# Batch 0's attention written out in a fixed order, with products on zeros in each step; batch 1 takes its mask from TensorE

## The chip, the cores and the metric

The kernel runs on one core of a Trainium2 chip. The metric is the device time in microseconds (us) of one execution, the median of several. The core has five engines that the text names: TensorE (PE in the rows; PEld is its weight load), VectorE (DVE), ScalarE (ACT), GpSimd (POOL) and SyncE (SP, which here only issues transfers). Each engine runs its own instructions in order and waits on semaphores for the others. TensorE's clock has two levels, 1.2 and 2.4 GHz; the profile gives the granted clock as a share of the upper one, so 0.50 is the lower level and 1.00 the upper.

## What is computed

Four batches of 576 tokens with eight heads of 64 channels go through attention, then through a dense network with a residual, then through a routed one with eight experts.

```python
scores = scale * np.matmul(q, k.transpose(0, 1, 3, 2))
mask_local = (rel >= 0) & (rel < 32)
mask_strided = (rel >= 0) & (pos[None, :] % 32 == pos[:, None] % 32)
scores = np.where(masks[None], scores, -1000000000.0)      # heads 0-3 local, 4-7 strided
attn = np.exp(scores - np.max(scores, axis=-1, keepdims=True))
attn = attn / (np.sum(attn, axis=-1, keepdims=True) + 1e-09)
x = np.matmul(attn, v)                                     # to tokens x 512 channels
xn = (x - mu) / np.sqrt(var + 1e-06) * g_ln
x = x + np.maximum(xn @ w_ch1, 0.0) @ w_ch2                # 512 -> 2048 -> 512
...                                                        # then one of 8 experts per token
```

## The kernel before, in words

Both masks leave few keys per query, so attention is cut into blocks. A *pair* is two heads of one batch, `(b, hp)`; its queries are handled in three *units* of three or four blocks. A unit goes through five stages, each a function of its own: `st_scores` (scores into PSUM, then what DVE does to them), `st_exp` (exponentials on ACT), `st_norm` (the division by the sum), `st_trans` (transposes on TensorE and a copy back to SBUF by ACT) and `st_out` (the product with v and the copy into `xt`, the input of the dense network). Before a pair's first unit, `prep` transposes its q and k and copies them into place. All PSUM tiles of these stages share four buffers through `side`.

The dense network takes its tokens in chunks of 256. Chunk 0 is the first 256 tokens of batch 0, so its first product (`mm1`, L613) needs all four pairs of batch 0. Batch 0's attention therefore stands at the front of the program, with nothing but preparation beside it: 12 units in the order `(0, 0)`, `(0, 2)`, `(0, 3)`, `(0, 1)`. The text calls it the prologue. Batches 1 to 3 are worked into the products of the dense network by a plan of due times (`SPANS`), batch 1 beside the chunks 0 and 1. The dense weights come as 64-bit numbers and are turned into pairs of 32-bit ones in *turns* (`w_low` and `w_high` on DVE, `w_sign` on ACT, `w_split` on DVE or ACT and POOL); six turns are worked into the prologue.

Batch 0 is the only one in `FAST`. For a fast unit the mask is a product of a unit matrix with the mask on TensorE (L300), DVE takes the largest score (L316) and subtracts it (L317), and ACT does one exponential for the unit (L328). The sum of the exponentials comes from two more products with a matrix of equal numbers (L372), after which DVE adds 1e-9 (L378), takes the reciprocal of all 162 to 216 columns (L379) and multiplies while it copies into `xt` (L397). For the other batches DVE adds the mask and finds the extreme in one operation per block (L320), ACT does one exponential with a running sum per block (L331), and DVE divides on the 3 or 4 sums of a row (L340 to L342).

`keep_clock` issues products whose results nobody reads: ten at the start (`WARM0`), on a block of zeros, and two of 256 columns in each unit of batch 0 (`WARM`), on the transposed weights `pt`:

```python
if b == 0:
    keep_clock(pt...[0:n, 0:256]..., WARM)
```

The order of instructions on an engine is the scheduler's, which works from the program text and its own estimates; `keep` and `issue_after` pin single ones. SP issues the transfers of batch 0 with those of the first six weight blocks between them (`load_mixed`, `ORD`): small v transfers alternate with large weight blocks.

## Time and profile before

| | |
|---|---|
| three executions | 914.50, 916.74, 918.66 us, median 916.74 |
| the profiled execution | 914.36 us |
| its span, first to last instruction | 912.5 us |
| mean granted clock of TensorE | 0.962 |
| busy of the span: PE, PEld, DVE, ACT, POOL | 96%, 86%, 52%, 40%, 17% |
| first product of the dense network | 71.90 us |

Lengths in rows overlap where an engine starts an instruction before the one ahead of it has ended, so the distance between two starts, and not the length, is what an instruction takes of its engine. A wait is named by what ended it.

### The profile page before, as it was taken

To read this page: it belongs to the slowest core of one execution; us is meant where nothing else is said; L and a number is where in the kernel's file an instruction comes from. 1 tells how busy PE (TensorE), PEld (TensorE's weight loads), DVE (VectorE), ACT (ScalarE), POOL (GpSimd) and SP (SyncE) were. 2 spreads that over 40 slices of the span, in tenths; PEclk is the share of its full clock that TensorE was granted. 3 is DMA by queue.
4 is the path that set the end of the run, shared out by engine and by line. 5 is a ranking of instruction groups with operands and counts; after the bars stand their busy time and mean duration, and the time that the engine had idled before them with its cause. 6 is when DMAs were issued, how large, how long until landed. Compare 5 with 4: busy or idle time off the path is not lost. (4 is left out here: it accounts for less than half of the span.)

```text
span 912.5 us, 18019 instructions
## 1 busy us (share of the span) xinstructions
PE 873.2 (96%) x6644; PEld 782.2 (86%) x6644; DVE 474.3 (52%) x1560; ACT 368.9 (40%) x919; POOL 152.2 (17%) x163
## 2 busy tenths in 40 slices
PE   7888899899999999999999999999999999999994
PEld 5657888899999999899999999999877787787773
DVE  3778756537775646657555464675722134111541
ACT  2448879943354423354231212242112244222551
POOL 2013323312020020120121212020131111110100
PEclk8757989999999999999999999999999999999999
DMA  9850444310222201210000000511374364510730
GB/s 218 219 188 1 117 108 133 91 48 1 74 52 62 57 2 27 68 43 17 28 2 24 2 24 1 185 49 47 139 265 143 139 224 157 194 48 24 285 114 15
DMA packets 95024, 82.92 MB, mean 91 GB/s; under 512 B 67395, under 2 KB 75589, under 8 KB 94920
## 3 DMA queue, kind: packets, MB, share of 16 engines
q1 hardware_dynamic: 87656, 65.41, 24.2%
q0 software_dynamic: 3632, 11.11, 3.6%
q10 hardware_dynamic: 3632, 5.09, 1.6%
q8 instruction: 55, 0.90, 0.4%
q14 instruction: 49, 0.40, 0.1%
HBM read 72.08 MB, written 10.30 MB: 90 GB/s over the span
## 5 line engine op out<-in xcount | busy, mean ns | idle before, releaser
L629 PE MATMUL acc<-h,w 128*128 128x256 f32 x1728 | 246.2, 290 | 1.0 <-DVE h L616 1.0
L613 PE MATMUL ps_h<-xc,w 128*128 128x256 f32 x1728 | 242.6, 288 | 2.5 <-ACT xc L596 1.7
L613 PEld LDWEIGHTS ps_h<-xc,w 128*128 128x128 f32 x1728 | 222.7, 195 | 5.8 <-ACT xc L596 2.4
L629 PEld LDWEIGHTS acc<-h,w 128*128 128x128 f32 x1728 | 219.9, 192 | 3.6 <-DVE h L616 1.4
L615 ACT ACTIVATE h<-ps_h 128x256 fp32r<-128x256 f32 x144 | 55.6, 386 | 220.6 <-PE ps_h L613 206.1
L616 DVE SCALAR_TENSOR_TENSOR h<-ps_h,h 128x256 fp32r<-128x256 f32 x144 | 60.7, 421 | 93.7 <-ACT h L615 93.3
L1341 PE MATMUL ps_h<-wx,xs 128*128 128x512 f32 x360 | 87.6, 398 | 0.8 <-DVEq L1268 0.8
L1369 PE MATMUL ps_y<-wx,ht 128*128 128x512 f32 x360 | 85.9, 394 | 0.0
L1341 PEld LDWEIGHTS ps_h<-wx,xs 128*128 128x128 f32 x360 | 66.6, 188 | 15.8 <-DVEq L1268 1.3
L1369 PEld LDWEIGHTS ps_y<-wx,ht 128*128 128x128 f32 x360 | 66.5, 188 | 13.3
L470 POOL TENSOR_TENSOR w<-stg,w 128x512 fp32r<-128x512 f32 x32 | 45.2, 1412 | 136.1 <-ACT w L469 69.6
L1372 ACT ACTIVATE y<-ps_y,pr 128x512 f32<-128x512 f32 x19 | 13.1, 688 | 89.2 <-PE ps_y L1369 61.6
L331 ACT ACTIVATE sm<-sm,st 108x54 f32<-108x54 f32 (+1 forms) x120 | 41.4, 348 | 15.5 <-DVE st L320 15.3
L449 ACT ACTIVATE stg<-stg 128x512 f16<-128x512 f32 x32 | 43.9, 1371 | 0.7 <-DVE stg L443 0.6
L867 DVE TENSOR_TENSOR xs<-ps_tx,xs 128x512 fp32r<-128x512 f32 x15 | 10.4, 691 | 64.0 <-ACTq L1268 45.8
L1344 ACT ACTIVATE h<-ps_h 128x512 f32<-128x512 f32 x30 | 16.3, 595 | 62.0 <-PE ps_h L1341 62.0
L759 DVE TENSOR_TENSOR wx<-raw,wx 128x1024 fp32r<-128x1024 f32 x32 | 37.5, 1220 | 1.7 <-ACT wx L756 1.3
L304 PE MATMUL ps_sc<-kT,qbd 128*128 128x96 f32 (+1 forms) x280 | 34.8, 263 | 1.6 <-DVE xt L399 0.7
L304 PEld LDWEIGHTS ps_sc<-kT,qbd 128*128 128x128 f32 (+1 forms) x280 | 32.2, 182 | 2.9 <-DVE xt L399 0.9
L756 ACT CAST wx<-raw 128x1024 fp32r<-128x1024 f32 x32 | 31.8, 1061 | 5.7 <-PE acc L629 4.1
L1373 POOL DMA_INDIRECT out_dram<-y,idx x15 | 15.1, 1005 | 113.0 <-ACT y L1372 71.3
L455 DVE SCALAR_TENSOR_TENSOR stg<-stg 128x512 int32<-128x512 int32 x32 | 25.1, 785 | 15.3 <-ACT stg L450 14.9
(375 smaller groups left out, 1203.9 us busy)
## 6 DMA issues: line engine op xcount, KB each, us to landing
stg<-in_moe_w_ch_dram SPq DMA_DIRECT2D x32, 512.0 KB
raw<-in_moe_w_dram SPq DMA_DIRECT2D x16, 1024.0 KB
raws<-in_moe_w_dram SPq DMA_DIRECT2D x16, 1024.0 KB
xrows<-row ACTq DMA_DIRECT2D x9, 520.0 KB
qnat<-in_q_dram SPq DMA_DIRECT2D x48, 72.0 KB
knat<-in_k_dram SPq DMA_DIRECT2D x48, 72.0 KB
v<-in_v_dram SPq DMA_DIRECT2D x24, 72.0 KB
v<-in_v_dram SPq DMA_DIRECT2D x72, 18.0 KB
```

The source lines that it names most:

```text
L304: pe.matmul(ps[0:m, i, :], qbd[:, q0:q0 + w, :].rearrange("p s j -> p (s j)"), kT[:, k0:k0 + n], start=not fast, stop=not fast or i == ng - 1)
L331: act.activation(sm[0:m, i, :], sm[0:m, i, :], AF.Exp, bias=st[0:m, 0, i:i + 1], scale=-1.0, accum_out=st[0:m, 1, i:i + 1])
L449: keep(act.activation(t.bitcast(F16)[..., 1], f32(t[..., 1]), AF.Copy, scale=2.0 ** -112))
L470: keep(pool.tensor_tensor(w[:, 1], r, f32(w[:, 0]), op=ALU.subtract))
L613: pe.matmul(ps, w[:, a, d, o:o + 128], xcs[c][:, b_, d, :], start=(i == 0), stop=(i == 11))
L615: act.activation(h[:, 0, :], ps, AF.Relu)
L616: dve.scalar_tensor_tensor(h[:, 1, :], ps, 0.0, f32(h[:, 0, :]), op0=ALU.max, op1=ALU.subtract)
L629: pe.matmul(accs[c][d // 2][:, d % 2, :], w[:, a, f % 2, d * 128:(d + 1) * 128], h[:, b_, :], start=(f == 0 and (a, b_) == (0, 0) and d % ...
L756: act.copy(wx[i][:, 0, :], raw[i // 2][:, i % 2, :])
L759: dve.tensor_tensor(wx[i][:, 1, :], raw[i // 2][:, i % 2, :], f32(wx[i][:, 0, :]), op=ALU.subtract)
L1341: pe.matmul(hp_[fg], s_[:, a, d, :], wx[d][:, b_, 512 * fg:512 * fg + 512], start=(i == 0), stop=(i == 11))
L1369: pe.matmul(ps, s_[a][:, f, :], wx[4 + f // 2][:, b_, 512 * (f % 2):512 * (f % 2) + 512], start=(i == 0), stop=(i == 23))
```

## The change

The prologue becomes a loop that is written out: 15 steps for 12 units. Step i issues the scores of unit i, the normalisation of unit i-1, the transposes of unit i-2, the output of unit i-3 and the exponentials of unit i, and in the steps 1, 2, 4, 5, 7 and 8 the q or k of the next pair. While `pinned` is set, every instruction of TensorE, ACT and DVE is kept in this order. Each step ends with five products of 512 columns on the block of zeros, six in the steps 0 to 2; the two per unit on `pt` are gone. The weight turns stand in the steps 6 to 11.

The sums of a unit with a TensorE mask are now one DVE reduction over the exponentials (`st_norm`), followed by the same short division as in the other batches; the two products per unit with equal numbers and the wide reciprocal are gone. Units of the pairs `(0, 0)` and `(0, 2)` have mode 2: ACT reads the scores from PSUM, one exponential per block with the extreme as bias, and DVE copies the output. Mode 1, for `(0, 3)`, `(0, 1)` and all of batch 1, keeps the subtraction on DVE and one exponential; in batch 0 ACT copies its output. The factor of the scores moves into the copy of q, in all batches, with its sign turned, so that DVE looks for the least. Transposes of q and k of batch 0 take the two PSUM buffers of the dense network. Batches 2 and 3 keep mode 0.

SP issues q, k and v pair by pair, the first two weight blocks after the third and fourth pair and the other four behind.

```diff
-FAST = (0,)
+MODES = {(0, 0): 2, (0, 2): 2, (0, 3): 1, (0, 1): 1, 1: 1}
...
-NEG = -1.0e9 / SCALE
+NEG = -1.0e9
...
-SMB, SM0, PT0, TL = 2, 3, 2, 1
-WARM0, WARM, LB = 10, 2, 5
+SMB, SM0, PT0, TL = 2, 4, 2, 1
+WARM0, WARM, LB = 10, 5, 5
...
-    pe, act, dve, pool, sp = nc.tensor, nc.scalar, nc.vector, nc.gpsimd, nc.sync
...
+        def __getattr__(self, name):
+            fn = getattr(self.eng, name)
+            if not pinned[0] or name == "dma_start":
+                return fn
+            return lambda *args, **kw: tc.keep_in_program_order(fn(*args, **kw))
+
+    pe, act, dve = Pin(nc.tensor), Pin(nc.scalar), Pin(nc.vector)
+    pool, sp = nc.gpsimd, nc.sync
...
-    pool.affine_select(out=mask_loc, in_=mask_loc, pattern=[[-2, 128]], compare_op=ALU.is_ge, fill=NEG, base=2 * STR, channel_multiplier=1)
...
+    pool.affine_select(out=mask_loc, in_=mask_loc, pattern=[[-2, 128]], compare_op=ALU.is_ge, fill=-NEG, base=2 * STR, channel_multiplier=1)
...
-            ps = side_r([128, 3 * QT], "ps_tr")
+            ps = (ps_m.tile([128, 512], F32, tag="m", name="ps_tr")[:, 0:3 * QT] if b == 0 else side_r([128, 3 * QT], "ps_tr"))
...
-                act.copy(dst(qbd[0:64, 0:S, 0]), s_[0:64])
...
+                act.activation(dst(qbd[0:64, 0:S, 0]), s_[0:64], AF.Copy, scale=-SCALE)
+                if half and b:
+                    act.activation(dst(qbd[64:128, 0:S, 1]), s_[64:128], AF.Copy, scale=-SCALE)
+                else:
+                    dve.tensor_scalar(dst(qbd[64:128, 0:S, 1]), s_[64:128], -SCALE, None, op0=ALU.mult)
...
-        fast = b in FAST
+        mode = mode_of(b, hp)
...
-        if fast:
+        if mode:
...
-        if fast:
-            mx = st[0:m, 0, 0:ng]
-            return [lambda: dve.tensor_reduce(mx, ps[0:m], axis=AX.X, op=ALU.max),
-                    lambda: dve.tensor_tensor(sm[0:m], ps[0:m], mx.unsqueeze(2).to_broadcast([m, ng, n]), op=ALU.subtract)]
+        sms[b, hp, u0] = (sm, st, ps)
+        mn = st[0:m, 0, 0:ng]
+        if mode:
+            new = [lambda: dve.tensor_reduce(mn, ps[0:m], axis=AX.X, op=ALU.min)]
+            if mode == 1:
+                new.append(lambda: dve.tensor_tensor(sm[0:m], ps[0:m], mn.unsqueeze(2).to_broadcast([m, ng, n]), op=ALU.subtract))
+            return new
...
-            dve.tensor_tensor_reduce(sm[0:m, i, :], ps[0:m, i, :], mask(i), -SCALE, 3.0e38, ALU.add, ALU.min, st[0:m, 0, i:i + 1])
+            dve.tensor_tensor_reduce(sm[0:m, i, :], ps[0:m, i, :], mask(i), 1.0, 3.0e38, ALU.add, ALU.min, st[0:m, 0, i:i + 1])
...
-        if b in FAST:
-            act.activation(sm[0:m], sm[0:m], AF.Exp, scale=SCALE)
+        mode = mode_of(b, hp)
+        if mode == 1:
+            act.activation(sm[0:m], sm[0:m], AF.Exp, scale=-1.0)
             return
         for i in range(ng):
-            act.activation(sm[0:m, i, :], sm[0:m, i, :], AF.Exp, bias=st[0:m, 0, i:i + 1], scale=-1.0, accum_out=st[0:m, 1, i:i + 1])
+            act.activation(sm[0:m, i, :], (ps if mode else sm)[0:m, i, :], AF.Exp, bias=st[0:m, 0, i:i + 1], scale=-1.0, **({} if mode else dict(accum_out=st[0:m, 1, i:i + 1])))
...
-        if b in FAST:
-            return []
-        return [
+        todo = [
             lambda: dve.tensor_scalar(rs, rs, 1e-9, None, op0=ALU.add),
             lambda: dve.reciprocal(rs, rs),
             lambda: dve.tensor_tensor(sm[0:m], sm[0:m], rs.unsqueeze(2).to_broadcast([m, ng, n]), op=ALU.mult),
         ]
+        if mode_of(b, hp):
+            todo.insert(0, lambda: dve.tensor_reduce(rs, sm[0:m], axis=AX.X, op=ALU.add))
+        return todo
...
-        ps = side([128, 2, ng, w] if fast else [128, 1, ng, w], "ps_o")
+        ps = side([128, ng, w], "ps_o")
...
-        if fast:
-            for j in range(2):
-                pe.matmul(ps[64 * j:64 * j + 64, 1], mean_w[0:n, 0:64], pt[0:n, :, j::2], start=True, stop=True)
-        if b == 0:
-            keep_clock(pt.rearrange("p g m -> p (g m)")[0:n, 0:256].bitcast(BF16).rearrange("p (n w) -> p n w", w=2)[:, :, 1], WARM)
...
-        if fast:
-            rs = pt.rearrange("p g m -> p (g m)")[:, 0:ng * w]
-            dve.tensor_scalar(rs, ps[:, 1].rearrange("p g q -> p (g q)"), float(DM), 1e-9, op0=ALU.mult, op1=ALU.add)
-            dve.reciprocal(rs, rs)
...
-            if fast:
-                dve.tensor_tensor(dst, cut(o), cut(rs), op=ALU.mult)
-            else:
-                (dve.tensor_copy if i % 2 else act.copy)(dst, cut(o))
+            (dve.tensor_copy if (i % 2 if b else mode_of(b, hp) > 1) else act.copy)(dst, cut(o))
...
-    def weights_next():
-        for fn, i in turns[nw[0]] + joins[nw[0]]:
+    def weights_turn():
+        for fn, i in turns[nw[0]]:
             fn(i)
         nw[0] += 1
+
+    joined = [0]
+
+    def weights_join():
+        while joined[0] < nw[0]:
+            for fn, i in joins[joined[0]]:
+                fn(i)
+            joined[0] += 1
+
+    def weights_next():
+        weights_turn()
+        weights_join()
...
-    load_qk(*pairs[0])
-    load_v0(0)
-    load_qk(*pairs[1])
-    big = [hold(load_w, 0), hold(load_w, 1), hold(load_qk, *pairs[2]), hold(load_w, 2), hold(load_w, 3), hold(load_qk, *pairs[3]), hold(load_w, 4), hold(load_w, 5)]
-    small = [hold(load_v0, i) for i in range(1, 4)]
-    for n in ORD:
-        load_mixed(sum((big[i] for i in n[0]), []), sum((small[i] for i in n[1]), []))
+    for i in range(4):
+        load_qk(*pairs[i])
+        load_v0(i)
+        if i > 1:
+            load_w(i - 2)
+    for i in range(2, W_START):
+        load_w(i)
...
-    while pos[0] < NSTEP or any(fifo.values()):
-        i = pos[0]
...
+    pinned[0] = True
+    us = [(b, hp, u0) for b, hp in pairs[:4] for u0, _ in GROUPS[hp]]
+    for nm in "qk":
+        prep(*pairs[0], nm)
+        keep_clock(idle, 2)
+    for i in range(len(us) + 3):
+        new, old = st_scores(*us[i]) if i < len(us) else [], st_norm(*us[i - 1]) if 0 < i <= len(us) else []
+        for p in old + new:
+            p()
+        if 1 < i < len(us) + 2:
+            st_trans(*us[i - 2])
+        if i > 2:
+            st_out(*us[i - 3])
+        if i < len(us):
+            st_exp(*us[i])
+        weights_join()
+        if i < 9 and i % 3:
+            prep(*pairs[i // 3 + 1], "qk"[i % 3 - 1])
+        keep_clock(idle, WARM + (i < 3))
+        if i > 2 and us[i - 3] == (0, 1, 0):
+            ln_0()
+        if i > 2 and us[i - 3] == (0, 1, 3):
+            ln0 = [ln_2, ln_split]
+        if i > WI and nw[0] < W_START:
+            weights_turn()
         if ln0:
             ln0.pop(0)(0)
+    weights_join()
+    pinned[0] = False
     pos[0] = NSTEP
```

What this does to the order, first on TensorE in the prologue, one unit of the pair `(0, 2)` (`ps_sc` scores, `ps_pt` transposes, `ps_o` output, `idle_ps` products that nobody reads). Before:

```order
L300 LDWEIGHTS iw
L300 MATMUL ps_sc<-mask_str,iw 108x216
L304 MATMUL ps_sc<-spare 108x54 x4
L350 MATMUL ps_pt<-iw,first 96x128 x3
L369 MATMUL ps_o<-first,v_174 64x64 x6
L372 MATMUL ps_o<-first,mean_w 64x192 x2
L285 LDWEIGHTS first
L285 MATMUL idle_ps<-first 128x256
```

With the change (line 84 is the wrapper that pins):

```order
L84 LDWEIGHTS iw
L84 MATMUL ps_sc<-mask_str,iw 108x216
L84 MATMUL ps_sc<-spare 108x54 x4
L84 MATMUL ps_pt<-iw,first 96x128 x3
L84 MATMUL ps_o<-first,v_174 64x64 x6
L84 LDWEIGHTS spare
L84 MATMUL idle_ps<-spare 128x512
```

The products with `mean_w` are gone, and what follows the output reads `spare`, the block of zeros, instead of `first`, which holds `pt`; four more such pairs follow.

On DVE, in the pair `(0, 3)` and after it (`st` sums and extremes, `xt` the output). Before:

```order
L378 TENSOR_SCALAR first<-ps_o 128x216
L317 TENSOR_TENSOR first<-ps_sc,st 128x288
L379 RECIPROCAL first<-first 128x216
L316 TENSOR_REDUCE st<-ps_sc 128x3
L397 TENSOR_TENSOR xt_331<-ps_o,first 128x12x8
L397 TENSOR_TENSOR xt_362<-ps_o,first 128x12x8
L397 TENSOR_TENSOR xt_387<-ps_o,first 128x12x2
L317 TENSOR_TENSOR first<-ps_sc,st 128x288
```

With the change:

```order
L84 TENSOR_REDUCE st<-first 108x4
L84 TENSOR_SCALAR st<-st 108x4
L84 RECIPROCAL st<-st 108x4
L84 TENSOR_TENSOR first<-first,st 108x216
L84 TENSOR_REDUCE st<-ps_sc 108x4
L84 TENSOR_TENSOR first<-ps_sc,st 108x216
L84 COPY xt_361<-ps_o 128x12x8
L84 COPY xt_397<-ps_o 128x12x8
L84 COPY xt_445<-ps_o 128x12x2
```

The wide reciprocal has gone; a reduction and two operations on four columns stand ahead of a product, and all of it comes before the next unit's scores are looked at.

On SP, behind the loads of the first pair, before:

```order
L191 DMA qk<-in_q_dram 96x6x64 x2
L191 DMA qk<-in_k_dram 96x6x64 x2
L191 DMA stg<-in_moe_w_ch_dram 128x4x256
L191 DMA v_189<-in_v_dram 18x11x64
L191 DMA stg<-in_moe_w_ch_dram 128x1024
L191 DMA v_189<-in_v_dram 18x11x64
L191 DMA qk<-in_q_dram 96x6x64
```

With the change, from the third pair on:

```order
L205 DMA qk<-in_q_dram 96x6x64 x2
L205 DMA qk<-in_k_dram 96x6x64 x2
L205 DMA v_196<-in_v_dram 18x11x64 x2
L205 DMA v_196<-in_v_dram 18x10x64
L205 DMA v_196<-in_v_dram 18x11x64 x2
L205 DMA v_196<-in_v_dram 18x10x64
L205 DMA stg<-in_moe_w_ch_dram 128x4x256
```

The q and k of the third pair stood behind two weight blocks and now stand ahead of all of them.

## Rows read from the trace of the kernel before

**Rows 1.** The page, busy tenths in 40 slices of the span: TensorE
```profile
PE   7888899899999999999999999999999999999994
```

**Rows 2.** Busy us of each engine by stretch, then granted clock, DMA share, GB/s
```profile
14.00:31.00 17.00, 16.14 (x107) 12.56 (x108) 8.17 (x18) 5.03 (x14) 0.00 (x0) 0.50 1.06 237
31.00:41.30 10.30, 8.83 (x107) 6.25 (x105) 7.92 (x22) 5.16 (x12) 0.00 (x0) 1.00 0.95 251
41.30:71.90 30.60, 25.58 (x167) 16.30 (x168) 24.46 (x51) 13.23 (x22) 5.65 (x4) 0.50 0.47 153
71.90:78.60 6.70, 6.36 (x24) 5.66 (x25) 6.40 (x13) 4.96 (x9) 1.64 (x1) 0.50 0.01 2
98.00:188.00 90.00, 80.88 (x718) 76.40 (x718) 53.01 (x202) 78.22 (x192) 29.92 (x23) 0.96 0.42 114
```

**Rows 3.** Timeline of TensorE before 80 us: start, length, line, operation, count
```profile
1.22 4.45 PE L285 MATMUL idle_ps<-spare 128*128 128x512 bf16 x10 [1.22 <-DVE spare L926]
...
7.26 0.30 PE L300 MATMUL ps_sc<-mask_loc,iw 128*128 128x96 bf16 x2
...
8.44 0.29 PE L300 MATMUL ps_sc<-mask_loc,iw 128*128 128x288 bf16 x1
...
9.21 0.29 PE L300 MATMUL ps_sc<-mask_loc,iw 128*128 128x288 bf16 x1
...
9.97 0.41 PE L265 MATMUL ps_tr<-iw,qk 96*128 96x96 f32 x3
...
48.27 0.42 PE L300 MATMUL ps_sc<-mask_loc,iw 128*128 128x288 bf16 x1
...
49.72 0.75 PE L350 MATMUL ps_pt<-iw,first 108*54 108x108 f32 x3
...
71.90 1.94 PE L613 MATMUL ps_h<-xc,w 128*128 128x256 f32 x6 [1.73 <-ACT xc L596]
```

**Rows 4.** Timeline of TensorE from 137 to 159 us
```profile
137.39 0.49 PE L350 MATMUL ps_pt<-iw,sm 128*96 128x128 f32 x3
137.72 0.81 PE L304 MATMUL ps_sc<-kT,qbd 128*128 128x96 f32 x6
...
147.25 0.66 PE L265 MATMUL ps_tr<-iw,qnat 96*128 96x96 f32 x6
147.69 1.07 PE L629 MATMUL acc<-h,w 128*128 128x256 f32 x7
...
158.25 0.57 PE L369 MATMUL ps_o<-pt,v 96*64 96x64 f32 x12
158.75 0.50 PE L613 MATMUL ps_h<-xc,w 128*128 128x256 f32 x2
```

**Rows 5.** Timeline of DVE, copy into the first 256 tokens
```profile
67.90 0.42 DVE L397 TENSOR_TENSOR xt<-ps_o,first 128x64 f32<-128x64 f32 x2
```

**Rows 6.** Groups by line and shape, 0 to 78 us: busy, mean ns, idle before
```profile
L379 DVE RECIPROCAL first<-first 128x192 f32<-128x192 f32 x6 | 8.1, 1344 | 0.1
...
L449 ACT ACTIVATE stg<-stg 128x512 f16<-128x512 f32 x6 | 8.2, 1358 | 0.1
...
L450 ACT ACTIVATE stg<-stg 128x512 f32<-128x512 f32 x6 | 4.0, 668 | 0.1
...
L316 DVE TENSOR_REDUCE st<-ps_sc 128x3 f32<-128x288 f32 x6 | 2.7, 447 | 2.8 <-PE ps_sc L304 2.8
...
L328 ACT ACTIVATE first<-first 128x288 f32<-128x288 f32 x6 | 2.5, 448 | 6.4 <-DVE first L317 6.4
```

**Rows 7.** Groups by line and shape, 78 to 440 us
```profile
L331 ACT ACTIVATE sm<-sm,st 128x96 f32<-128x96 f32 x54 | 19.8, 370 | 11.4 <-DVE st L320 11.2
...
L331 ACT ACTIVATION_READ_ACCUMULATOR sm<-sm,st 128x1 f32 x54 | 10.3, 191 | 0.0
...
L342 DVE TENSOR_TENSOR sm<-sm,st 128x288 f32<-128x288 f32 x18 | 8.2, 453 | 0.2
...
L340 DVE TENSOR_SCALAR st<-st 128x3 f32<-128x3 f32 x18 | 3.9, 215 | 7.6 <-ACT sm L331 7.1
```

**Rows 8.** Waits of TensorE from 98 to 188 us, longest in total first
```profile
PE ps_tr L265 <- DVE qbd L277: 2.8, 2, 2.3
PE ps_o L369 <- ACT pt L358: 1.3, 1, 1.3
PE ps_var L549 <- ACT pt L358: 1.2, 1, 1.2
```

More of the change, by code (lines that the diff above doesn't have):

```diff
@@ L72, in attention_moe_moe, with __init__ @@
     nc = tc.nc
-    pe, act, dve, pool, sp = nc.tensor, nc.scalar, nc.vector, nc.gpsimd, nc.sync
+    pinned = [False]
+    class Pin:
+        def __init__(self, eng):
+            self.eng = eng
+        def __getattr__(self, name):
[5 more added lines that the diff above has]
+    pool, sp = nc.gpsimd, nc.sync
     def f32(ap):
@@ L275, in prep @@
             else:
-                act.copy(dst(qbd[0:64, 0:S, 0]), s_[0:64])
-                (act.copy if half and b else dve.tensor_copy)(dst(qbd[64:128, 0:S, 1]), s_[64:128])
+                act.activation(dst(qbd[0:64, 0:S, 0]), s_[0:64], AF.Copy, scale=-SCALE)
[3 more added lines that the diff above has]
+                    dve.tensor_scalar(dst(qbd[64:128, 0:S, 1]), s_[64:128], -SCALE, None, op0=ALU.mult)
     sms, pts = {}, {}
@@ L303, in st_scores @@
             k0 = max(0, q0 - STR) if hp < 2 else q0
-            pe.matmul(ps[0:m, i, :], qbd[:, q0:q0 + w, :].rearrange("p s j -> p (s j)"), kT[:, k0:k0 + n], start=not fast, stop=not fast or i == ng - 1)
+            pe.matmul(ps[0:m, i, :], qbd[:, q0:q0 + w, :].rearrange("p s j -> p (s j)"), kT[:, k0:k0 + n], start=not mode, stop=not mode or i == ng - 1)
         if b == 0:
@@ L368, in st_out @@
             for j in range(2):
[L369 to L379 removed]
+                pe.matmul(ps[64 * j:64 * j + 64, i, 0:k], vv[0:min(n, k) if hp > 1 else n, i, j, :], pt[0:min(n, k) if hp > 1 else n, i, j:2 * k:2], start=True, stop=True)
+        o = ps.rearrange("p g q -> p (g q)")
         i = 0
```

40 lines of the change are left out of this document (8 added, 32 removed).

## The prediction

> **What bounds the kernel now.** I read the page first. From the ninth of its 40 slices on, some 180 us after the start, TensorE is busy all the time, and only the earlier slices fall below that [rows 1], so whatever brings forward the dense network's first product brings forward the end by about as much. That product starts at 71.90 us [rows 3]. Next the table by stretch [rows 2], where two things stand. TensorE's clock was granted at the lower level, 1.2 GHz, from 14 to 31 us and again from 41.3 to 78.6 us, and at the upper, 2.4 GHz, only in the 10 us between; and in the low stretches it was busy 16.1 of 17 and 25.6 of 30.6 us. So the prologue is bound by TensorE at half clock for the larger part, and by DVE in the rest (24.5 of 30.6 us). The groups by line show what DVE spends itself on: the wide reciprocal takes 1.34 us of each of six units [rows 6], and the others are as wide. Last I read the stretch of batch 1, 98 to 188 us: TensorE idles there for 9.1 of 90 us while ACT is busy 78.2 [rows 2], and its longest waits are for ACT and DVE [rows 8]. After that it hardly idles.
>
> **Term 1, the prologue.** The new loop has 15 steps in a fixed order, so I work out how long a step is for each engine, with the clock at the upper level.
>
> TensorE: the mask product and the scores of a unit take 0.77 us from one mask product to the next [rows 3], the transposes 0.33, six transposes of a q or k 0.44, the output 0.50 [rows 4]. The five products on zeros have no row at the upper level. Ten of them took 4.45 us at the start [rows 3], 0.445 each, which is 512 columns at 1.2 GHz; at 2.4 GHz I take half, 0.22, so 1.1 per step. Sum 2.7, with a q or k 3.15.
>
> The loop between DVE and ACT: DVE looks for the extreme (0.447 [rows 6]), ACT takes three exponentials (at most 0.370 each, the row that also keeps a running sum [rows 7]), DVE reduces over them, then two operations on three columns and a product. The reduction over SBUF has no row; it lies between the short operation's 0.215 and the product's 0.453 [rows 7], and I take the 0.447 of the same shape in PSUM. The reciprocal on three columns I take like the other short one. That is 0.45 + 1.11 + 0.45 + 0.22 + 0.22 + 0.45 = 2.9. In mode 1 a subtraction and one exponential of 0.448 [rows 6] replace the three: 2.7.
>
> ACT in the steps 7 to 11, where a weight turn lies: sign work 1.36 + 0.67 [rows 6], the exponential 0.45, the copy of the transposes and two or three output copies, for which I take four times 0.3, bounded by 0.2 and 0.45 from the short and the long operations above: 3.7, or 3.3 with the lower bound.
>
> The three engines lie within 2.7 and 3.7 of each other, and none waits for another inside one step, since the transposes and outputs belong to older units. I take 3.3 us a step; the range is 2.8 (nothing but the loop) to 4.1 (ACT's 3.7 and a wait ahead of it).
>
> The first mask product stood at 7.26 us [rows 3]; four products on zeros are put ahead of it, 0.9, so 8.2. Twelve steps reach 47.8, step 12 reaches 51.1. In step 13 the transposes, the output and a copy (0.33 + 0.50 + 0.32) bring the last of the first 256 tokens at 52.3. From there to the first dense product I take what it takes now, from the end of the copies at 68.3 [rows 5] to 71.9, which is 3.6, and 0.4 because five products on zeros now stand ahead of the mean on TensorE: 56.3. **That is 15.6 us less**; with the bounds of a step, 13 of which lie on the path, it is between 5.2 (4.1 us each) and 22.1 (2.8 us each).
>
> What else is moved costs nothing as long as its cover holds. SP: the DMA share is full until 31 us at some 240 GB/s [rows 2]; q, k and v of batch 0, 3.5 MB, so land by about 17 us and the six weight blocks (0.52 MB each) by about 30, as today. The first weight block is wanted in step 6 (28 us) and lies behind three pairs only; the last is wanted in step 11 (44 us). The tightest are q and k of the second pair, wanted in step 1 at about 11 us; in the trace their transposes start at 9.97 without a wait for a transfer [rows 3], and the same loads stand ahead of them as before. If that cover were gone, TensorE would stand still behind them, as the order is pinned. The factor in q's copy changes no count of operations, in batches 2 and 3 it lies beside a TensorE that is never idle: nothing.
>
> **Term 2, the clock at the first dense products.** They ran at the lower level for 6.7 us [rows 2]. TensorE's 6.4 busy us could halve, 3.2 less; but DVE is busy 6.4 us of the same stretch and the first products wait for its halves of the input. Between 0 and 3.2 I take 1.0, nearer to DVE's row.
>
> **Term 3, batch 1.** ACT loses 40 exponentials with a running sum (0.370 + 0.191 each [rows 7], 22.4 us) and gets 12 of 0.448, 5.4 us: 17 less of its 78.2. DVE gets about as much as it loses. TensorE gets 14 mask products, whose price I bound by nothing (hidden in the idle time) and the 0.29 of their length [rows 3]: 1.8 us is taken. Of the 9.1 us of idle time some 2.8 hang on DVE's copy of q and the rest mostly on ACT [rows 8]; I take that 4 go. Net 2 us less, from 7 less to 4 more.
>
> **The sum.** 914.36 - 15.6 - 1.0 - 2.0 = 895.8 against the profiled execution's own time. That execution lies 2.4 us under the median of 916.74, so I forecast a median of **898 us**.
>
> **The clock as the trace shows it, and a rule.** All of term 1 stands on the upper level. In the trace the ten full products at the start were followed by the upper level (0.29 for 288 columns at 8.44, against 0.42 at 48.27 [rows 3]). It fell at 14 us after TensorE had stood waiting for copies, and then stayed low through 17 us in which TensorE was busy 95% of the time, though with products of 54 to 96 columns on parts of the array [rows 2]. The new products are as wide as those at the start and take a third of each step, which none of the low stretches has. The Trainium skill (TensorE: Matmul & The Clock Gate, Part 1) says that the throttled state is the default and that sustained activity releases it. By that rule a TensorE that is busy throughout would win the clock back soon whatever it computes, so the second rival below could not last. This trace disagrees: 14 to 31 us was busy and low.
>
> **The rivals.**
>
> *The order costs more than it hides* (0.13). With everything pinned, one late copy holds an engine that has other work ready, as the scheduler's freedom is gone. For it: the three engines lie close together, so a slip of one is a slip of all. Against it: each stage has a step of slack. Steps of 4.1 us give 8.2 + 13 x 4.1 + 5.2 = 66.7 for the first product, 5.2 less than now: about 908.5.
>
> *The clock stays low for most of the prologue, and the products on zeros become the bound* (0.06): this is the slower side. At 1.2 GHz scores with their mask take 1.45 (48.27 to 49.72 [rows 3]), the transposes up to 0.75, the output and the six transposes up to twice the above (1.0 and, in half of the steps, 0.9), the five products 2.2: 5.6 a step, 2.3 more than at the upper level. The gain of 15.6 is gone when 7 of the 15 steps run low; all 15 give 34.5 more, so 19 us slower in the prologue, less 2 for batch 1: 934. For it: the trace has two long low stretches under a busy TensorE. Against it: the width of the new products.
>
> *The clock falls once, in the weight steps* (0.08), where steps grow to ACT's 3.7 and the last units have no scores: seven low steps eat term 1, batch 1 still gives 2 or 3, so about 914: no change.
>
> *Batch 1 gives all its idle time back* (0.10): 9 less there and not 4, and 3.2 in term 2: about 891, or 888 if the steps reach 3.1.
>
> That the change does nothing is no rival: the wide reciprocal and the products for the sums do leave the order.
>
> **How the numbers follow.** The forecast has 0.63, spread over 892 to 905 by the bounds of a step; the first and last rival lie at its two ends. The range of 887 to 910 holds the forecast, most of the last rival and most of the first: 0.8 or a little more. A measurement of this kernel tells some 0.5%, 4.6 us, from no change. Faster by more than that: 0.63 + 0.13 + 0.10 = 0.86. Within it: 0.08. Slower: 0.06.
>
> **What would show it.** Right: a granted clock near 1.00 from 10 us to the first dense product, that product at 54 to 59 us, mask products of the prologue about 3.3 us apart, less idle time of TensorE in the stretch of batch 1, and the rest unchanged in length. Wrong: mask products 5 us or more apart at 0.50 (second rival), 4 us apart at 1.00 with TensorE waiting for ACT or DVE (first rival), or a first product at 56 us with its gain lost later, while weights are being turned.

## The result and the profile after

The changed kernel takes 902.17 us (median of four executions, 900.97 to 903.65) against 916.94 us before (four, 914.50 to 918.66): ratio 0.9842, 95% interval 0.9813 to 0.987. The forecast was 898 us with a range of 887 to 910: the sign and the range hold, and the gain is 14.8 us where 18.6 were summed up. In a later comparison the same kernel took 907.4 us (six executions, 903.0 to 908.86), ratio 0.9878 with interval 0.9839 to 0.9916; why it varies is one of the findings below.

The profiled execution took 902.98 us, its span is 901.2 us and the mean granted clock 0.983. On the page, the rows that answer to [rows 1], TensorE and its clock:

```profile
PE   8989888999999999999999999999999999999995
...
PEclk9999999899999999999999999999999999999997
```

The table by stretch, to be read against [rows 2]; the columns are the same. The first call:

```profile
14.00:31.00 17.00, 15.44 (x153) 10.85 (x151) 11.81 (x42) 7.67 (x26) 0.00 (x0) 1.00 1.07 266
31.00:41.00 10.00, 10.00 (x112) 7.58 (x112) 9.14 (x29) 7.72 (x17) 1.40 (x1) 1.00 0.99 260
41.00:57.00 16.00, 13.05 (x120) 8.12 (x117) 12.91 (x29) 11.24 (x27) 4.24 (x3) 1.00 0.50 159
```

In this profile the clock stays at its upper level through the whole prologue, where it stood at 0.50 for 17 and then 30.6 us before [rows 2]. TensorE's timeline shows the steps (all pinned instructions have the line of the helper, L84) and the first dense product, now L636:

```profile
8.37 0.29 PE L84 MATMUL ps_sc<-mask_loc,iw 128*128 128x96 bf16 x2
...
16.12 0.26 PE L84 MATMUL ps_sc<-mask_str,iw 108*108 108x216 bf16 x1
...
17.93 0.93 PE L84 MATMUL ps_sc<-spare 128*108 128x54 f32 x8 [1.55 <-ACT spare L84]
...
20.72 0.26 PE L84 MATMUL ps_sc<-mask_str,iw 108*108 108x216 bf16 x1
...
42.95 0.29 PE L84 MATMUL ps_sc<-mask_loc,iw 128*128 128x288 bf16 x1
...
48.28 0.53 PE L84 MATMUL ps_pt<-iw,first 128*96 128x128 f32 x3 [1.89 <-DMA stg<-in_moe_w_ch_dram]
...
56.91 3.41 PE L636 MATMUL ps_h<-xc,w 128*128 128x256 f32 x24
```

From the first mask product at 8.37 to the twelfth at 42.95 lie 11 steps, 3.14 us each. The first dense product starts at 56.91 us instead of 71.90 [rows 3]: 15.0 us earlier. The span shrank by 11.3 us only, so something is given back behind it. To find where, I counted the products into `ps_h`, the tile of that product (2152 in each trace, the first 1728 of them of L613 before and L636 now), and compared the start of the 1st, the 73rd and the 289th. The table has the experiments too; they are told below. A ratio is to runs of the kernel before in the same comparison, of which there were four (the change; e1 to e4; e5 to e8; e9 to e12).

| kernel | 1st, us | 73rd | 289th | 73rd to 289th | ratio to before, 95% interval |
|---|---|---|---|---|---|
| before | 71.90 | 97.58 | 190.29 | 92.7 | 1 |
| changed | 56.91 | 78.85 | 177.14 | 98.3 | 0.9842 [0.9813, 0.987] |
| changed, again (e11) | 59.18 | 81.12 | 179.27 | 98.2 | 0.9878 [0.9839, 0.9916] |
| e1 no products on zeros in the steps | 62.78 | 86.19 | 184.38 | 98.2 | 0.9907 [0.9884, 0.993] |
| e3 before, with products on zeros | 65.28 | 91.67 | 185.19 | 93.5 | 0.9932 [0.9908, 0.9956] |
| e5 order left to the scheduler | 62.83 | 84.78 | 182.69 | 97.9 | 0.9889 [0.9857, 0.992] |
| e6 sums of batch 0 as before | 62.79 | 86.29 | 182.58 | 96.3 | 0.9896 [0.9854, 0.9938] |
| e4 transfers in the old order | 59.18 | 81.13 | 179.27 | 98.1 | 0.9864 [0.9844, 0.9885] |
| e2 batch 1 as before | 57.26 | 79.20 | 168.95 | 89.8 | 0.9813 [0.9787, 0.9839] |
| e7 no added 1e-9 | 54.44 | 76.36 | 168.53 | 92.2 | 0.9755 [0.9724, 0.9786] |
| e9 the same, batch 0 alone | 54.10 | 76.06 | 177.63 | 101.6 | 0.9812 [0.9779, 0.9845] |
| e10 the same, batch 1 alone | 57.21 | 79.14 | 176.26 | 97.1 | 0.9816 [0.9777, 0.9854] |
| e8 e2 and e7 together | 54.46 | 76.39 | 167.07 | 90.7 | 0.9748 [0.9715, 0.9781] |
| e12 e8, k of the second pair by DVE | 53.68 | 75.59 | 167.65 | 92.1 | 0.9715 [0.9683, 0.9748] |

Against before, the lead of the changed kernel is 15.0 us at the 1st product, 18.7 at the 73rd, 13.15 at the 289th, up to 14.3 between that and the last one, and 13.19 there. So the later stages pass on about what lead there is; another 1.9 us are lost behind the last of them. There TensorE waits 2.05 us for ACT in both kernels, and the 24 products that follow take longer now, first before, then changed:

```profile
892.91 5.73 PE L1369 MATMUL ps_y<-wx,ht 128*128 128x512 f32 x24
```

```profile
879.72 7.34 PE L1395 MATMUL ps_y<-wx,ht 128*128 128x512 f32 x24
```

These 24 products take 5.7 us in eight of the fourteen profiles and 7.1 to 7.3 in six; e3, the kernel before with products on zeros, is one of the six, and e4 is not. So most of the 1.9 us is a fall of the clock that comes in some executions, and no part of the change.

One caution for what follows: the prologue of the changed kernel stands unaltered in e2, e10 and e11, with the first product at 57.26, 57.21 and 59.18 us. One prologue so varies by 2.3 us from one execution to the next.

What is won and lost lies in three places: the prologue (-15.0), the first 72 products (25.7 us before, 21.9 now: -3.7), and the stretch in which batch 1's attention and the turning of the weights lie beside the products (92.7 before, 98.3 now: +5.6).

### The profile page after: what moved, and what is told of

The parts are those of the page before. It is cut to its first block, busy times and chain, and to the rows that moved or that the text cites. A ratio compares the mean times of both kernels' runs of the same rounds, so it can differ in the third digit from the quotient of the medians.

```text
span 901.2 us, 17965 instructions
## 1 busy us (share of the span) xinstructions
PE 867.3 (96%) x6668; PEld 777.3 (86%) x6668; DVE 474.5 (53%) x1520; ACT 365.6 (41%) x879; POOL 152.2 (17%) x163
## 5 line engine op out<-in xcount | busy, mean ns | idle before, releaser
L636 PE MATMUL ps_h<-xc,w 128*128 128x256 f32 x1728 | 239.6, 287 | 0.0
L636 PEld LDWEIGHTS ps_h<-xc,w 128*128 128x128 f32 x1728 | 221.6, 194 | 1.7
L639 DVE SCALAR_TENSOR_TENSOR h<-ps_h,h 128x256 fp32r<-128x256 f32 x144 | 60.6, 421 | 94.2 <-ACT h L638 93.5
L460 ACT ACTIVATE stg<-stg 128x512 f16<-128x512 f32 x27 | 37.2, 1377 | 0.6 <-DVE stg L454 0.6
L354 ACT ACTIVATE sm<-sm,st 108x54 f32<-108x54 f32 (+1 forms) x80 | 27.6, 347 | 13.5 <-DVE st L342 13.4
L1384 DVE TENSOR_TENSOR ht<-ps_th,ht 128x512 fp32r<-128x512 f32 x30 | 19.3, 685 | 24.5 <-ACT ht L1383 24.1
L324 PE MATMUL ps_sc<-kT,qbd 128*108 128x54 f32 (+1 forms) x240 | 30.5, 267 | 0.0
L892 DVE SCALAR_TENSOR_TENSOR pr<-io_e,e_rep,xg 128x8 f32<-128x8 f32 x15 | 3.4, 226 | 51.2 <-ACT y L1398 46.0
```

The lines of the kernel that those rows point to most:

```text
L324: pe.matmul(ps[0:m, i, :], qbd[:, q0:q0 + w, :].rearrange("p s j -> p (s j)"), kT[:, k0:k0 + n], start=not mode, stop=not mode or i == ng - 1)
L354: act.activation(sm[0:m, i, :], (ps if mode else sm)[0:m, i, :], AF.Exp, bias=st[0:m, 0, i:i + 1], scale=-1.0, **({} if mode else dict(acc ...
L460: keep(act.activation(t.bitcast(F16)[..., 1], f32(t[..., 1]), AF.Copy, scale=2.0 ** -112))
L636: pe.matmul(ps, w[:, a, d, o:o + 128], xcs[c][:, b_, d, :], start=(i == 0), stop=(i == 11))
L639: dve.scalar_tensor_tensor(h[:, 1, :], ps, 0.0, f32(h[:, 0, :]), op0=ALU.max, op1=ALU.subtract)
```

## The experiments

### The prologue: clock, order and sums

**e1: no products on zeros in the steps.**

```diff
-        keep_clock(idle, WARM + (i < 3))
```

> The changed kernel without the products on zeros inside its steps (the ten at the start and the four between the first transposes stay); nothing else differs. Theory A (the clock): the steps are short because these products hold TensorE at the upper level. Without them the granted clock is 0.50 for most of 12 to 60 us; a step on TensorE is then 1.45 (scores and mask at the lower level) + 0.75 + 1.0 + half of 0.9 = 3.65 us, up to 4.1, and the first dense product comes at 62 to 68 us instead of 56.9: ratio 0.990 to 0.996. Rival B (the order): the fixed order and the shorter DVE work make the gain, and the products on zeros only take 1.1 us a step from TensorE. Then the clock stays high or a step stays at 3.3 us, the first dense product comes at 57 us or before, and the ratio is 0.984 or lower.

Measured: 908.07 us, ratio 0.9907, first dense product at 62.78. The table by stretch of this run:

```profile
14.00:31.00 17.00, 13.83 (x99) 11.80 (x97) 9.43 (x32) 6.88 (x23) 0.00 (x0) 0.52 1.04 260
31.00:41.00 10.00, 10.00 (x86) 8.69 (x84) 7.34 (x28) 5.19 (x11) 0.00 (x0) 0.50 1.06 278
41.00:57.00 16.00, 14.40 (x100) 11.61 (x99) 15.35 (x35) 12.53 (x27) 5.64 (x4) 0.50 0.32 92
```

Theory A: the clock is low from 14 us on, and stays low through 10 us in which TensorE never pauses. But only 5.9 of the 15.0 us go (3.6 if e11's 59.18 is taken for the changed kernel); 9.1 remain at the lower clock.

**e3: the kernel before, with products on zeros.**

```diff
-    def keep_clock(t, n):
+    def keep_clock(t, n, pin=lambda x: x):
...
-            pe.matmul(idle_ps[:, 0:t.shape[-1]], t[:, 0:128], t, start=True, stop=True)
+            pin(pe.matmul(idle_ps[:, 0:t.shape[-1]], t[:, 0:128], t, start=True, stop=True))
...
-            keep_clock(pt...[0:n, 0:256]..., WARM)
+            keep_clock(idle, 5, tc.keep_in_program_order)
```

> The kernel before, with one edit: behind each of batch 0's outputs five pinned products on zeros of 512 columns in the place of the two of 256 columns on the transposed weights. Theory A (the clock): the granted clock is near 1.00 from about 25 us on to the first dense product. The order and DVE's wide reciprocals stay, and DVE's 0.8 busy share in the low stretch bounds what comes of it: the first dense product at 63 to 67 us instead of 71.9, ratio 0.990 to 0.995. Rival B (the order): the clock is not what holds this prologue, and 12 times five products of 0.22 to 0.45 us, less the 24 left out, put 10 us or more on TensorE: the first product at 75 us or later, ratio 1.003 or more.

Measured: 911.83 us, ratio 0.9932, first dense product at 65.28, 6.6 us earlier than before. Two rows of its table by stretch:

```profile
31.00:41.00 10.00, 9.49 (x107) 6.49 (x107) 8.78 (x21) 4.18 (x10) 0.00 (x0) 1.00 0.80 220
41.00:57.00 16.00, 13.86 (x137) 8.76 (x134) 15.23 (x36) 8.97 (x15) 2.84 (x2) 1.00 0.82 233
```

In these two stretches the clock is as high as in the changed kernel (from 14 to 31 us it was 0.80), and DVE is busy 15.2 of the last 16 us: now the old sums bind. Rival B, that such products only cost, falls: they are worth 6.6 us in the old order (e3) and 3.6 to 5.9 in the new (e1).

**e5: only the products on zeros pinned, the rest left to the scheduler.**

```diff
-            pe.matmul(idle_ps[:, 0:t.shape[-1]], t[:, 0:128], t, start=True, stop=True)
+            tc.keep_in_program_order(pe.matmul(idle_ps[:, 0:t.shape[-1]], t[:, 0:128], t, start=True, stop=True))
...
-    pinned[0] = True
+    pinned[0] = False
```

> The changed kernel with nothing of batch 0 pinned but the products on zeros; the scheduler orders the rest on every engine. Theory of the forecast: the fixed order is what keeps a step at 3.3 us; the first rival said it costs more than it hides. So far: products on zeros alone took 6.6 us off the first dense product, order and arithmetic without them 9.1. If the fixed order is most of those 9.1, this run has its first dense product at 61 to 65 us and a ratio of 0.988 to 0.994. Rival: the shorter DVE work and not the order is what counts; then it stands at 55 to 59 us and the ratio at 0.981 to 0.987.

Measured: 906.93 us, ratio 0.9889, first dense product at 62.83: 5.9 us later than with the fixed order (3.6 against e11), as the first theory has it. The longest wait of TensorE in this prologue shows one thing that the fixed order does:

```profile
PE ps_tr L279 <- DMA qk<-in_q_dram: 4.2, 1, 4.2
```

The scheduler has put transposes of a later pair ahead of other work, and TensorE stands 4.2 us until their q has landed. The changed kernel has no such wait in its prologue. The clock falls about this wait too (0.70 on the mean from 14 to 31 us), so this run doesn't part the order from the clock: what it loses holds both.

**e6: the sums of batch 0 as before, in the new order.**

```diff
-MODES = {(0, 0): 2, (0, 2): 2, (0, 3): 1, (0, 1): 1, 1: 1}
+MODES = {0: 1, 1: 1}
...
+                pe.matmul(po[64 * j:64 * j + 64, 1], mean_w[0:n, 0:64], pt[0:n, :, j::2], start=True, stop=True)
...
+            dve.reciprocal(rs, rs)
...
+                dve.tensor_tensor(dst, cut(o), cut(rs), op=ALU.mult)
```

> The changed kernel with batch 0's softmax sums as before: TensorE's two products per unit against a constant, DVE's wide scale and reciprocal and the product with it at each output copy; order, products on zeros and loads as changed, every unit with DVE's subtraction and one exponential. DVE then has in a step 0.45 + 0.45 for extreme and subtraction, 0.3 to 0.45 for the scale, 1.34 for the reciprocal and two or three products of 0.25 to 0.45 each: 3.4 to 3.9, and beside q's copies and weights up to 4.8. If DVE's arithmetic bounds the prologue: first dense product at 61 to 66 us, ratio 0.988 to 0.995. Rival: the order alone hides DVE's longer work: first product at 56 to 59 us, ratio 0.983 to 0.987.

Measured: 907.59 us, ratio 0.9896, first dense product at 62.79. The row of its late steps:

```profile
41.00:57.00 16.00, 13.16 (x122) 7.71 (x119) 15.52 (x35) 8.82 (x13) 4.76 (x4) 1.00 0.79 241
```

The clock is up and DVE is full (15.5 of 16 us): DVE's arithmetic binds, the rival falls. The pairs `(0, 0)` and `(0, 2)` also get DVE's subtraction back, so this tries DVE's arithmetic as a whole, and not the sums alone.

So with any one of the three parts taken away, about 9 us of the prologue's gain remain. Each costs 5.9 us of 15.0 by the first profile and 3.6 of 12.7 by e11; the three sum to more than the whole by the one and to less by the other, so whether a part is worth more beside the other two is not shown.

**e4: transfers in the order of before.** The list of loads is that of the kernel before, with `load_mixed` and `ORD`.

```diff
-    for i in range(4):
-        load_qk(*pairs[i])
...
+    for n in ORD:
+        load_mixed(sum((big[i] for i in n[0]), []), sum((small[i] for i in n[1]), []))
```

> The changed kernel with the transfers issued in the order of before (weight blocks 0 to 3 ahead of and between the third and fourth pair of q and k). By the forecast the new order of loads is worth nothing: every block lands ahead of the step that wants it, so the ratio stays at 0.984 (0.981 to 0.987) and the first dense product at 57 us. Rival: in a pinned order a late transfer stops everything behind it; the third pair lands 4 us later and v of the second pair with it, TensorE waits for transfers in steps 3 to 8, the clock may fall there, and the first product comes 1 to 6 us later: 0.986 to 0.992.

Measured: 904.09 us, ratio 0.9864, first dense product at 59.18, with the clock at 0.90 from 14 to 31 us. By itself this looked like a cost of 2.3 us, though TensorE waits for no transfer in it. But e11, the changed kernel again, has its first product at the same 59.18 and the ratio 0.9878. The new order of loads is worth nothing that these runs can show.

### Batch 1, and one short operation

**e2: batch 1 as before.**

```diff
-MODES = {(0, 0): 2, (0, 2): 2, (0, 3): 1, (0, 1): 1, 1: 1}
+MODES = {(0, 0): 2, (0, 2): 2, (0, 3): 1, (0, 1): 1}
```

> The changed kernel with batch 1's mask, extreme and sums as they were before (one DVE operation adds the mask and finds the extreme, ACT's exponentials keep the sums); batch 0 is as changed. Theory of the forecast's third term: the new form of batch 1 is worth 2 us, so without it the ratio rises from 0.984 to 0.986 or 0.987, and TensorE waits more for ACT between 57 and 180 us. Rival: in the changed kernel the stretch from the first dense product to the 289th of its line took 120.2 us against 118.4 before, and its longest wait there, 2.3 us, is for the product that ends DVE's new chain of reduce, add, reciprocal and product; so the new form gives back what it saves on ACT. Then the old form of batch 1 is as fast or faster: ratio 0.979 to 0.984, and that stretch takes 116 to 119 us.

Measured: 900.26 us, ratio 0.9813 (five executions, 895.02 to 902.68; the profiled one is the fastest). The intervals of this and of the changed kernel overlap, so the times alone don't settle it; the stretch from the 73rd to the 289th product does. One row each, before, changed, and e2:

```profile
97.58:190.29 92.71, 83.59 (x749) 78.92 (x748) 54.38 (x206) 79.49 (x195) 30.47 (x23) 0.96 0.42 116
```

```profile
78.85:177.14 98.29, 88.41 (x756) 82.92 (x754) 65.26 (x162) 73.86 (x130) 32.03 (x24) 0.91 0.40 116
```

```profile
79.20:168.95 89.75, 81.74 (x742) 76.77 (x740) 57.17 (x206) 79.73 (x196) 31.66 (x24) 0.98 0.44 125
```

With the new form ACT is less busy by 5.6 us and DVE more by 10.9; TensorE idles 9.9 us instead of 9.1, and its clock is lower, so its work itself takes longer. In the table above the stretch takes 89.8 to 93.5 us in all five profiles with the old form (before, e2, e3, e8, e12) and 96.3 to 101.6 in eight of the nine with the new form; only e7, which drops a short operation, has 92.2. On the mean of these profiles that is 97.5 us with the new form and 91.7 with the old: it costs some 6 us there. Only 0.8 us of the changed kernel's loss is idle time of TensorE. An estimate from the granted clock has most of the rest: 0.91 over 98.3 us and 0.96 over 92.7 are about 18 and 7 us at the lower level, and 10 us more at half speed are 5 us. What the new form does to DVE is to be seen in its groups by line over this stretch (line, operation, count, then busy us and mean ns of one), first before, then changed:

```profile
L342 DVE TENSOR_TENSOR sm<-sm,st 128x288 f32<-128x288 f32 (+2 forms) x12 | 5.0, 416 | 0.3
```

```profile
L363 DVE TENSOR_TENSOR sm<-sm,st 128x288 f32<-128x288 f32 (+2 forms) x12 | 9.6, 804 | 0.3
...
L366 DVE TENSOR_REDUCE st<-sm 128x3 f32<-128x288 f32 (+2 forms) x12 | 4.8, 402 | 4.2 <-ACT sm L351 4.2
...
L361 DVE TENSOR_SCALAR st<-st 128x3 f32<-128x3 f32 (+2 forms) x12 | 2.6, 219 | 0.3
```

The same product takes 804 ns where it took 416: seven of the twelve now start while POOL is subtracting weights, and these take 0.62 to 1.59 us; before, none took over 0.46. And it ends TensorE's longest wait of the stretch in the changed kernel:

```profile
PE ps_pt L374 <- DVE sm L363: 2.3, 1, 2.3
PE ps_o L392 <- ACT pt L382: 1.8, 2, 1.0
```

That this product and this wait bring the clock down is not shown. e7 below keeps both, and its stretch is short and its clock up:

```profile
76.36:168.53 92.17, 83.96 (x755) 78.96 (x754) 64.29 (x150) 73.38 (x130) 31.55 (x24) 0.96 0.43 122
```

```profile
L362 DVE TENSOR_TENSOR sm<-sm,st 128x288 f32<-128x288 f32 (+2 forms) x12 | 9.9, 826 | 0.3
```

```profile
PE ps_pt L373 <- DVE sm L362: 2.2, 1, 2.2
```

**e7: without the addition of 1e-9.** A sum holds the exponential of its own extreme, which is 1, so adding 1e-9 changes no float32 value.

```diff
-            lambda: dve.tensor_scalar(rs, rs, 1e-9, None, op0=ALU.add),
```

> The changed kernel without the addition of 1e-9 to the softmax sums, in all four batches (a sum is at least 1, so that it changes no float32 value). It takes one short DVE operation per unit, 0.17 us and up to 0.9 beside POOL's weight split, out of the chain from the exponentials to the transposes. Theory: in the steps from 8 on and in batch 1 that chain is what TensorE waits for, so the first dense product comes 0.5 to 1.5 us earlier, the waits for DVE in batch 1 shrink, and the ratio goes from 0.984 to 0.979 to 0.983. Rival: the operation lies beside other waits (ACT's turns of weights): ratio 0.983 to 0.986.

Measured: 893.89 us (six executions, 893.38 to 897.0), ratio 0.9755: 8.3 us less than the changed kernel's 902.17 (13.5 less than its 907.4 in e11), more than expected. What the operation did in the prologue is to be seen in the changed kernel's timeline of DVE and POOL at the late steps:

```profile
45.92 0.42 DVE L84 TENSOR_SCALAR stg<-stg 128x512 int32<-128x512 int32 x1
46.08 1.41 POOL L481 TENSOR_TENSOR w<-stg,w 128x512 fp32r<-128x512 f32 x1 [2.73 <-DVE w L84]
46.25 0.45 DVE L84 TENSOR_REDUCE st<-first 128x3 f32<-128x288 f32 x1
46.73 0.78 DVE L84 TENSOR_SCALAR st<-st 128x3 f32<-128x3 f32 x1
...
47.55 0.18 DVE L84 RECIPROCAL st<-st 128x3 f32<-128x3 f32 x1
...
47.76 0.46 DVE L84 TENSOR_TENSOR first<-first,st 128x288 f32<-128x288 f32 x1
```

On three columns it takes 0.78 us, ending with POOL's subtraction at 47.5. The answer for the tile of the sums (least, median and greatest ns of one) has its other lengths:

```profile
L84 DVE TENSOR_SCALAR st<-st x12: 169/171/921, 11.2 to 50.9; 128x3 f32<-128x3 f32 x6, 108x4 f32<-108x4 f32 x4, 108x3 f32<-108x3 f32 x2
```

So 0.17 is the rule, and 0.78 to 0.92 what it takes in the four steps in which it starts while POOL is subtracting. In batch 1's stretch (78.85 to 177.14 us) it takes 0.16 to 0.17 us in eleven of twelve cases. DVE's whole step here, from 44.00 to 48.14, is 4.14 us. Without it (e7) the product meets POOL in its place, and the wait of TensorE at this point shrinks from 1.89 to 0.95 us. (The changed kernel's row at 48.28 names a transfer for it, but the transposes read what DVE's product finished at 48.22, and e2, e4 and e10 name DVE for the same wait.)

```profile
44.44 1.41 POOL L480 TENSOR_TENSOR w<-stg,w 128x512 fp32r<-128x512 f32 x1 [2.31 <-DVE w L84]
...
45.09 0.18 DVE L84 RECIPROCAL st<-st 128x3 f32<-128x3 f32 x1
...
45.31 0.86 DVE L84 TENSOR_TENSOR first<-first,st 128x288 f32<-128x288 f32 x1
...
46.22 0.53 PE L84 MATMUL ps_pt<-iw,first 128*96 128x128 f32 x3 [0.95 <-DVE first L84]
```

**e9 and e10: the same in batch 0 alone (below), in batch 1 alone (`b == 1`).**

```diff
+        if b == 0:
+            todo.pop(0)
```

> The changed kernel without the addition of 1e-9 in batch 0 alone. Leaving it out everywhere gave 8.3 us, of which the prologue shows 2.5 (first dense product at 54.4 instead of 56.9). Theory: the prologue's 2.5 are batch 0's and the rest batch 1's, ratio 0.980 to 0.983. Rival: the rest is not the operation's length either but where the batch 1 work falls after an earlier start: then this run has it all, 0.974 to 0.978.

> The changed kernel without the addition of 1e-9 in batch 1 alone; first dense product at 56.9 us as in the changed kernel. Theory: batch 1's shorter chain is worth the other 5 to 6 us, through fewer falls of the clock between 57 and 180 us: ratio 0.977 to 0.980. Rival: it is worth nothing there (ACT and the weights set the pace): 0.982 to 0.986.

Measured: 900.9 us for each, ratios 0.9812 and 0.9816, beside 0.9878 for the changed kernel in the same comparison (e11). So each gives about 0.006, and both together about the 0.012 that e7 (from the other comparison) has against e11; but the intervals of both overlap that of e11, so neither is clear by itself. e9's ratio is the one that its theory gave, and the prologue's 2.8 us are there (54.10). In its profile they are lost again behind the 73rd product (101.6 us), but that execution is the slowest of its six (903.83, the others 899.38 to 901.18). e10's ratio lies between its two theories.

**e8: batch 1 as before and no addition of 1e-9.**

> The changed kernel with batch 1's old form (as in the run with ratio 0.981) and without the addition of 1e-9 to the sums in all batches. If both gains are of the same kind (a shorter chain from scores to transposes keeps TensorE from waiting, and so the clock up), they add: ratio 0.975 to 0.980. If the addition costs nothing, 0.979 to 0.984.

Measured: 893.23 us, ratio 0.9748, beside e7's 0.9755 in the same comparison: not told apart. It was expected that the two gains add; e7 alone has as much as both. Once the addition is gone, these runs tell no difference between the forms of batch 1. Why, is not shown.

**e11: the changed kernel again**, without an edit.

> The changed kernel again, beside the next three. In its first profile the products 217 to 288 of the first dense line took 35.8 us, with the clock down to 0.50 there, against 30 to 32 in every other profile. If that is a fixed collision of this order, it stands here again: 35 us or more, ratio 0.981 to 0.987. If it is chance, the stretch takes 30 to 33 us, and the profiled execution comes out at 895 to 898 us.

Measured: 907.4 us, ratio 0.9878, first dense product at 59.18. The slow part that the first profile had between the 217th and the 289th product (35.8 us) is not there (32.3), so it is no fixed part of this order, though e9's profile has it again (35.9). But the execution is no faster, and the 895 to 898 us expected of it did not come: the clock fell elsewhere (0.90 from 14 to 31 us, 0.93 from the 73rd to the 289th product). TensorE's timeline at the wait that the changed kernel had at 48.28:

```profile
49.82 0.53 PE L84 MATMUL ps_pt<-iw,first 128*96 128x128 f32 x3 [1.89 <-DMA stg<-in_moe_w_ch_dram]
...
50.87 2.31 PE L84 MATMUL idle_ps<-spare 128*128 128x512 bf16 x5
```

and the same place in the first profile:

```profile
49.25 1.25 PE L84 MATMUL idle_ps<-spare 128*128 128x512 bf16 x5
```

After the same wait of 1.89 us, five products on zeros take 2.31 us here and 1.25 there: the clock fell in one execution and not in the other. In e2, e4 and e10, behind the same wait, they take 2.18, 2.31 and 2.31, so the first profile is the exception.

**e12: e8, and DVE instead of ACT copies k of the second pair.**

```diff
-                (act.copy if b == 0 else dve.tensor_copy)(dst(kT[:, 0:S]), s_)
+                (dve.tensor_copy if b or (b, hp) == pairs[1] else act.copy)(dst(kT[:, 0:S]), s_)
```

> The fastest so far (batch 1's old form, no addition of 1e-9; ratio 0.9748) with both copies of k of batch 0's second pair by DVE, which idles there, instead of ACT. TensorE waits 1.3 us for them in step 3. Theory: 0.6 to 0.9 us of that wait go and the first dense product comes as much earlier, 53.6 to 53.9 us, ratio 0.973 to 0.975. Rival: the loop of DVE and ACT has slack enough to swallow it: first product at 54.4 us, no difference.

Measured: 891.89 us (six executions, 890.51 to 892.87), ratio 0.9715: the lowest time of all, 25.3 us under the kernel before in the same comparison (917.18). The wait in step 3 went from 1.3 to 0.6 us and the first product from 54.46 to 53.68, as its theory says. Its ratio's interval (0.9683 to 0.9748) overlaps that of e8, so that the whole kernel gained by it is not shown.

## Why the prediction was right, and where it was not

**Term 1, the prologue: right in size.** Forecast 15.6 us less with the first dense product at 56.3, measured 15.0 and 56.91 (12.7 in e11). The first mask product was put at 8.2 and stood at 8.37; a step of 3.3 us was taken, and 3.14 came out. In part that is luck, for two errors cancel: the twelfth mask product stood at 42.95, 1.6 us ahead of the 44.5 that the sum gives, and from there to the first dense product it took 14.0 us where 11.8 were summed up. Two readings behind it were wrong. First, the working said that none of the engines waits for another inside a step; TensorE waits 1.55 us for ACT's copies of k in step 3 and 1.89 and 0.72 us for DVE later (rows at 17.93, 48.28 and 52.52 us). Second, it gave the longest late steps to ACT (3.7 us). It is DVE that fills them, 4.14 us, because the loop of 2.7 to 2.9 us left out three operations of each weight turn (0.68, 0.43 and 0.42 us) and priced the short addition at 0.22, where beside POOL it takes 0.78. These steps are few, so the sum survived.

**"All of term 1 stands on the upper level": wrong.** e1 keeps 9.1 of the 15.0 us at a clock of 0.50. A step at the lower level without products on zeros is short enough: e1's mask products from 20.57 to 47.67 us are 3.9 us apart. The second rival's 5.6 us a step had counted 2.2 for those products (and its own terms make 5.85 where a q or k is counted in half of the steps). The weighing of the rule against the trace holds: the Trainium skill (TensorE: Matmul & The Clock Gate, Part 1) says that sustained activity releases the throttle, and e1 shows TensorE busy 10.00 of 10.00 us from 31 to 41 us at 0.50.

**Term 2, the first dense products: mis-sized.** Forecast -1.0 with a bound of 3.2; the first 72 products took 3.7 us less. They started at the upper level and not at the lower, and TensorE was busy for all of the 15 us from 57 us on, so the bound that was taken from DVE's row did not hold. Nor is it the clock alone: in this profile it fell for 3.4 us at 64.6 us, in e11 it stood at 1.00 throughout, and the stretch took 21.9 us in both.

**Term 3, batch 1: the step that failed.** Forecast -2.0 with a bound of +4; measured +5.6 in the profile and +5.4 in e11; by the means of all profiles the new form costs some 6 us. Two readings were wrong. The 17 us that ACT was to lose are the lengths of rows that overlap (its exponentials and the reads of their sums, 21.6 us before and 4.8 now); busy time fell by 5.6 only. The groups from the 73rd to the 289th product, first before, then changed:

```profile
L331 ACT ACTIVATE sm<-sm,st 108x54 f32<-108x54 f32 (+1 forms) x40 | 13.8, 349 | 1.6 <-DVE st L320 1.4
...
L331 ACT ACTIVATION_READ_ACCUMULATOR sm<-sm,st 108x1 f32 (+1 forms) x40 | 7.8, 195 | 0.0
```

```profile
L351 ACT ACTIVATE sm<-sm 128x288 f32<-128x288 f32 (+2 forms) x12 | 4.8, 402 | 3.8 <-DVE sm L338 3.8
```

And "DVE gets about as much as it loses" left out that DVE's new chain meets POOL: DVE gained 10.9 us of busy time, and TensorE's longest wait is now for its product. So the 4 us of idle time that were to go did not (9.1 us before, 9.9 now), and the clock, for which the term had nothing, fell for some 10 us more. What brings it down there stays open. Of the sum of -18.6, terms 2 and 3 were to give -3.0, and gave +1.9 (-3.7 and +5.6). With the prologue's -15.0 and the 1.9 us at the end, that is the 11.3 us of the two spans.

**The rivals.** The first (steps of 4.1) came true in the last steps alone. The clock did not fall in the first profile's prologue, but did in e11's, at 19.9 and at 50.6 us for 3.4 us each, and not for seven steps. That batch 1 gives all its idle time back (888 to 891) is ruled out for this change; what comes near it is e12, which takes batch 1's new form and the short addition out.

**What would show it wrong** was named as "a first product at 56 us but its gain lost later, while weights are being turned": this is what happened to a third of it (5.6 of the 18.7 us that the lead had come to).

## What to carry to other kernels

When an engine's arithmetic is exchanged for another's, follow the chain that a waiting engine sees, not the lengths that go away: 17 us less of ACT's rows were 5.6 us less of its busy time, and TensorE idled no less. Look at what a short operation stands beside: one on three columns took 0.78 instead of 0.17 us beside POOL. Dropped everywhere it was worth 8 us in 902, of which only the 2.5 us in the prologue are traced to that. And where TensorE's clock can fall, a wait costs more than its length; shorten the waits of 1 to 2 us first, and judge by several executions, since a profile shows one throw.

## What the runs showed of the hardware

**DVE beside POOL.** DVE's addition on 3 columns takes 0.17 us, and 0.78 beside POOL's 1.41 us subtraction of a weight block; the product on 288 columns takes 0.46 and 0.86. The reduction of the same data in the same place keeps its 0.45. It matters which starts first: of batch 1's twelve products in the changed kernel's stretch, the seven that start while a subtraction is running take 0.62 to 1.59 us, and the four that start with it or up to 0.1 us ahead keep 0.33 to 0.39. The Trainium skill (SBUF — State Buffer, Who interferes with whom) describes the pair of ports that DVE and POOL share as a lock that the later one waits for. It names operations with two inputs in SBUF, as the product is, and lists the addition's kind among those that can take the pair; both rows agree.

**The clock after a wait.** The changed kernel's ten executions have mean granted clocks of 0.973 to 0.988 and times of 900.97 to 908.86; e12's six have 0.988 to 0.994 and 890.51 to 892.87. In the prologue of five profiles (the first, e2, e4, e10, e11) TensorE waits about 1.6 and 1.9 us; the first wait was followed by the lower level in two of them and the second in four. In the four kernels that had cut them to 1.4 us or less (e7, e8, e9, e12) the granted clock stayed at 1.00 through the prologue. The wait of 2.05 us at the end of the program was followed by the lower level in six of the fourteen profiles. And in the first profile the clock fell at 64.6 us, where TensorE had been busy without a pause since 57 us. Which of the waits between the 73rd and the 289th product lets the clock fall there, was not tried: the runs tell that the falls differ from one execution to the next, not which wait is to blame.
